# The scores of a chunk in 32 small matrix products of 64 rows by 32 columns instead of 16 of 64 by 64

## The chip, the cores and the metric

The kernel runs on one core of a Trainium2 chip. A core has a matrix engine (TensorE; PE in the profile, with PEld for its weight loads), three engines for element work (VectorE is DVE, ScalarE is ACT, GpSimd is POOL), and DMA queues, here issued by SyncE (SP). Matrix products read both operands from on-chip memory and write to PSUM, which has eight banks. The metric is device microseconds of a whole execution, lower is better; the median of several runs is given.

TensorE's array is 128 rows by 128 columns. A product whose stationary operand is smaller uses a part of it, called a place below: 64 rows by 64 columns makes four places, 64 rows by 32 columns eight. Which place a product takes follows from the partitions of its operands (rows) and of its result (columns). Products in different places can run at the same time. Each 32-bit product is issued as two passes, and each pass is one weight load and one matmul in the profile, so the counts of the profile are twice those of the code.

## The reference, cut to what matters

A decayed scan over 768 positions (4 batches, 8 heads, head size 32, state size 16) is followed by a feed-forward part. What the change touches is the scores `CB`:

```python
log_a = np.log(np.clip(a, 1e-06, 1.0))
for c in range(nc):
    cum = np.cumsum(la, axis=-1)
    L = np.exp(cum[:, :, :, None] - cum[:, :, None, :]) * causal
    CB = np.einsum('bhin,bhjn->bhij', Cc, Bc)
    M = CB * L
    y_intra = np.einsum('bhij,bhjd->bhid', M, xc)
    y_inter = np.einsum('bhin,bhnd->bhid', Cc, state) * decay_to_i[:, :, :, None]
    y[:, :, sl] = y_intra + y_inter
    state = decay_full[:, :, None, None] * state + np.sum(Bx, axis=2)
...
x = y.transpose(0, 2, 1, 3).reshape(B * S, H * D)
a = x @ w1
b = x @ w2
return (a * b @ w3) @ w_out
```

## The kernel before, in words

The scan runs over 16 chunks of 48 positions (`T = 48`). The state's 16 rows and a chunk's 48 positions are put together into blocks of 64 rows, so that one product per head gives the output and the next state at once. A chunk c has these steps on the engines:

- `c.CB`: the scores. 16 products, each with 64 rows (two heads' B with the unit matrix, zero elsewhere) and 64 of the 128 columns of a packed tile `bc`, against 96 columns of C. Row half r goes to PSUM bank `b[r]`; each product fills 64 partitions and 96 columns of it. In the profile: `ps<-bc`, 64*64, 32 matmuls.
- `c.M0`, `c.M1`: VectorE multiplies the two banks by the decays and leaves the result in `r`.
- `c.MX`: the sums, x and decays: 32 products of 64 rows by 32 columns, `r` against `xe`, 64 columns each. In the profile: `ps<-r,xe`, 64*32, 64 matmuls.
- `c.hi`, `c.lo`, `c.T` and `c.Z0` to `c.Z7` take the result out of PSUM: to `xT` for the feed-forward part, and the state's rows into the next chunk's `xe`.

Beside them the feed-forward part runs: `l<slice>.<block>.m` are the products with w1 and w2 (matmuls `ps<-xT,wh` and `ps<-xT,wl` of the whole 128 by 128 array), `v...M` multiplies w3 with w_out (`ps<-fr`), `d....m` are the last products (`ps<-wo,fr`). Products of 512 zeros (`ps<-zero`, the words with a `+`) fill TensorE early on.

The order of all work on every engine is written out by hand in the table `PLAN` (lines 25 to 82): each word is a task, with its engine behind a colon and its PSUM banks behind an @. Every operation is pinned to that order, by helpers on lines 134 to 150, so all matmuls show as L135 in the profile. In that order six `CB` stand right behind an `MX` on TensorE, three right in front of one, three behind another `CB`, and four between other products.

Of the kernel before, what the change touches and what calls it, by code (L numbers as in the profile page):

```python
# [85 lines left out]
def kernel(  # L86
# [17 lines left out]
    P = 128  # L104
# [18 lines left out]
    _, NST, NMAG, _, NOB, NCT, NR, NPK = 28, 4, 5, 11, 2, 2, 2, 3  # L123
# [7 lines left out]
    def sb(shape, dtype, name):  # L131
        return const.tile(shape, dtype, name=name)

    def mm(*args, **kw):
        pin(nc.tensor.matmul(*args, **kw))  # L135

    def load(dst, src, e="D"):
        pin((nc.scalar if e == "S" else nc.sync).dma_start(dst, src))  # L138
# [14 lines left out]
    psum = [PS[:, i] for i in range(8)]  # L153
# [23 lines left out]
    zero = sb([P, 512], BF16, "zero")  # L177
# [33 lines left out]
    tasks = {}  # L211

    def task(name):
        def put(f):
            tasks[name] = f
            return f
        return put
# [49 lines left out]
    def chunk(c):  # L267
# [3 lines left out]
        def step(name):  # L271
            return task(f"c{c}.{name}")
# [17 lines left out]
        if c < DIRECT:  # L290
            if c >= TRI:
                @step("K")
                def _(e, b):
                    q, k = divmod(c, SQ // T)
                    src = cq[q, :, :, :, k * T:(k + 1) * T]
                    load(LD.bitcast(F32)[RJ:, :, N:], src.rearrange("h g t s -> (g t) h s"), e)
                    for h2 in range(2):
                        load(RD.bitcast(F32)[RI + 2 * h2:RI + 2 * h2 + 2], src[h2].rearrange("g t s -> t g s"), e)
# [35 lines left out]
        def half(i):  # L334
            return psum[i][:, :HG * T]
# [14 lines left out]
            step(f"W{hf}")(lambda e, b, hf=hf: bw(hf))  # L350
            step(f"M{hf}")(lambda e, b, hf=hf: weigh(hf))

        @step("CB")
        def _(e, b):
            for r in range(2):
                v["pc", r] = half(b[r]).rearrange("p (g s) -> p g s", s=T)
            for k in range(4):
                for r in range(2):
                    rows = slice(64 * r, 64 * r + 64)
                    for i in range(2):  # L360
                        cols = slice(64 * i, 64 * i + 64)
                        mm(psum[b[r]][cols, 2 * T * k:2 * T * (k + 1)], bq[rows, k, cols], bq[rows, k, P:],
                           start=True, stop=True)


        @step("MX")
        def _(e, b):
            assert b[1] == b[0] + 1
            py = v["py"] = PS[:, b[0]:b[0] + 2].rearrange("p c (j k m) -> p (c j) k m", j=2, k=KT)[:, :, :, :TE]
            for kt in range(KT):  # L370
                for j in range(2):
                    for i in range(2):
                        for q in range(4):
                            n = 2 * (i ^ (q & 1)) + j
                            g = n * HP + 2 * kt + q // 2
                            rows = slice(64 * i, 64 * i + 64)
                            mm(py[32 * q:32 * q + 32, n, kt, :], xe[rows, g], R[rows, g, :], start=True, stop=True)

        if c + 1 < NCH:
            @step("T")  # L380
# [38 lines left out]
    for c in range(NCH):  # L419
        chunk(c)  # L420
# [165 lines left out]
            down(sl, t, vs)  # L586

    for word in PLAN.split():
        name, _, banks = word.partition("@")
        name, _, engine = name.partition(":")  # L590
        b = [int(i) for i in banks.split(",")] if banks else []
        if name[0] == "+":
            for _ in range(int(name[1:])):
                mm(psum[b[0]], zero[:, 0:P], zero, start=True, stop=True)
        else:
            tasks.pop(name)(engine, b)
    assert not tasks, list(tasks)


# [73 lines left out]
```

## Time and profile before

| | us |
|---|---|
| median of 3 runs (lowest to highest) | 276.61 (275.95 to 276.85) |
| the profiled execution's own time | 277.0 |
| its span in the profile | 275.2 |
| TensorE busy with matmuls (3024) | 267.5 (97%) |
| TensorE busy with weight loads (3026) | 236.6 |
| VectorE busy | 171.1 |
| ScalarE busy | 112.6 |
| GpSimd busy | 103.0 |

The 277.0 us of the profiled execution are 1.8 us more than its span, for start and end, and 0.4 us above the median. In rows of the timeline the first number is the start in us from the span's start, the second the time from there to the end of the last instruction of the row, so that the next row may start before it ends; xN is the number of matmuls in it. The granted clock was full (1.0) for the whole span.

### The profile page before, as it was taken

To read this page: it belongs to the slowest core of one execution; us is meant where nothing else is said; L and a number is where in the kernel's file an instruction comes from. 1 tells how busy PE (TensorE), PEld (TensorE's weight loads), DVE (VectorE), ACT (ScalarE), POOL (GpSimd) and SP (SyncE) were. 2 spreads that over 40 slices of the span, in tenths; PEclk is the share of its full clock that TensorE was granted. 3 is DMA by queue.
4 is the path that set the end of the run, shared out by engine and by line. 5 is a ranking of instruction groups with operands and counts; after the bars stand their busy time and mean duration, and the time that the engine had idled before them with its cause. 6 is when DMAs were issued, how large, how long until landed. Compare 5 with 4: busy or idle time off the path is not lost.

```text
span 275.2 us, 7389 instructions
## 1 busy us (share of the span) xinstructions
PE 267.5 (97%) x3024; PEld 236.6 (86%) x3026; DVE 171.1 (62%) x339; ACT 112.6 (41%) x242; POOL 103.0 (37%) x139
## 2 busy tenths in 40 slices
PE   8989999999999998999999999999999999999994
PEld 2459999999788897988988989988898899899994
DVE  4389997898896979988537462184447404441260
ACT  4484687755655442365143142042525212220220
POOL 3232527526445335465426061042416603250100
PEclk9999999999999999999999999999999999999999
DMA  6999979995983872606008100100211001000101
GB/s 193 344 272 318 307 254 319 269 293 161 376 247 111 289 249 79 182 0 183 18 23 243 48 21 0 50 28 0 63 58 39 2 27 52 0 0 23 39 19 40
DMA packets 21755, 36.05 MB, mean 131 GB/s; under 512 B 3672, under 2 KB 13528, under 8 KB 21720
## 3 DMA queue, kind: packets, MB, share of 16 engines
q1 hardware_dynamic: 21720, 35.56, 41.2%
q8 instruction: 24, 0.39, 0.6%
q14 instruction: 11, 0.09, 0.1%
HBM read 32.11 MB, written 3.44 MB: 129 GB/s over the span
## 4 chain that ended last, share of the span: by engine, by line
PE 88%; DMA 5%; DVE 2%; SPq 2%; issue 1%; ACT 0%
PE ps L135 88%; DMA xe<-in_x_dram 3%; SPq L138 2%; DMA st<-in_w3t_dram 1%; DMA st<-in_w_dram 1%; DVE mag L450 1%; DVE st L144 0%; DVE xT L141 0%; ACT xT L147 0%; DVE fr L141 0%; ACT gs L147 0%; DVE ob L147 0%; DVE wh L147 0%; DVE fr L147 0%; DVE gs L141 0%
## 5 line engine op out<-in xcount | busy, mean ns | idle before, releaser
L135 PE MATMUL ps<-xT,wh 128*128 128x512 f32 (+2 forms) x448 | 124.7, 362 | 1.0 <-DVE xT L141 1.0
L135 PEld LDWEIGHTS ps<-xT,wh 128*128 128x128 f32 x448 | 79.8, 188 | 11.5 <-DVE xT L141 1.0
L135 PE MATMUL ps<-xT,wl 128*128 128x512 f32 (+2 forms) x224 | 80.4, 359 | 0.0
L135 PE MATMUL ps<-wo,fr 128*128 128x256 f32 x576 | 69.7, 281 | 0.0
L135 PEld LDWEIGHTS ps<-wo,fr 128*128 128x128 f32 x576 | 68.7, 189 | 0.7
L141 POOL TENSOR_TENSOR fr<-gs,fr 128x512 fp32r<-128x512 f32 (+2 forms) x30 | 38.0, 1283 | 79.0 <-PE ps L135 29.0
L147 ACT COPY gs<-ps 128x512 f32<-128x512 f32 (+2 forms) x56 | 29.4, 524 | 65.1 <-PE ps L135 63.4
L141 DVE TENSOR_TENSOR gs<-gs,ps 128x512 f32<-128x512 f32 (+2 forms) x56 | 33.8, 608 | 33.8 <-PE ps L135 26.2
L135 PEld LDWEIGHTS ps<-xT,wl 128*128 128x128 f32 x224 | 42.2, 188 | 5.2
L147 DVE CAST fr<-gs 128x512 fp32r<-128x512 f32 (+2 forms) x29 | 13.4, 471 | 25.3 <-PE ps L135 24.7
L135 PE MATMUL ps<-fr 128*128 128x256 f32 x192 | 25.5, 286 | 0.8 <-DVE fr L141 0.8
L135 PEld LDWEIGHTS ps<-fr 128*128 128x128 f32 x192 | 24.1, 190 | 1.8 <-DVE fr L141 1.0
L141 POOL TENSOR_TENSOR fr<-mag,fr 128x512 fp32r<-128x512 f32 x11 | 15.9, 1445 | 17.9 <-DVE fr L147 14.8
L147 ACT COPY ob<-ps 128x256 f32<-128x256 f32 x16 | 6.0, 374 | 40.0 <-PE ps L135 34.7
L150 ACT ACTIVATE mag<-st 128x512 f32<-128x512 f32 x28 | 18.6, 674 | 8.2 <-DVE fr L141 5.4
L147 POOL COPY xe<-z 16x128 f32<-16x128 f32 x42 | 13.8, 330 | 20.1 <-DVE z L382 13.9
L141 POOL TENSOR_TENSOR r<-bn,r 128x128 f32<-128x128 f32 x32 | 16.0, 516 | 13.8 <-ACT r L150 8.5
L141 DVE TENSOR_TENSOR fr<-gs,fr 128x512 fp32r<-128x512 f32 (+2 forms) x26 | 19.5, 765 | 1.1 <-ACT fr L147 0.9
L450 DVE SCALAR_TENSOR_TENSOR mag<-mag,st 128x512 uint32<-128x512 uint32 x28 | 19.8, 717 | 0.2
L144 DVE TENSOR_SCALAR st<-st 128x512 uint32<-128x512 uint32 x28 | 14.5, 520 | 6.2 <-DMA st<-in_w_dram 4.1
L147 ACT CAST fr<-gs 128x512 fp32r<-128x512 f32 (+2 forms) x27 | 13.8, 559 | 10.5 <-PE ps L135 8.0
L141 DVE TENSOR_TENSOR r<-ps,r 128x384 f32<-128x384 f32 x32 | 16.6, 551 | 1.6 <-POOL r L141 0.8
(52 smaller groups left out, 209.8 us busy)
## 6 DMA issues: line engine op xcount, KB each, us to landing
st<-in_w3t_dram SPq DMA_DIRECT2D x16, 512.0 KB, 4.9
bc<-in_Ct_dram SPq DMA_DIRECT2D x14, 448.0 KB, 8.5
xe<-in_x_dram SPq DMA_DIRECT2D x16, 256.0 KB, 4.5
st<-in_w_dram SPq DMA_DIRECT2D x16, 256.0 KB, 6.2
ct<-cd SPq DMA_DIRECT2D x16, 192.0 KB, 6.2
out_dram<-ob SPq DMA_DIRECT2D x24, 128.0 KB, 2.1
st<-in_w_out_dram SPq DMA_DIRECT2D x4, 512.0 KB, 6.0
bn<-in_Bn_dram SPq DMA_DIRECT2D x14, 128.0 KB, 4.4
```

Of the source, the lines that this page charges most:

```text
L135: pin(nc.tensor.matmul(*args, **kw))
L138: pin((nc.scalar if e == "S" else nc.sync).dma_start(dst, src))
L141: pin((nc.gpsimd if e == "G" else nc.vector).tensor_tensor(*args))
L144: pin(nc.vector.tensor_scalar(*args))
L147: pin(nc.scalar.copy(*args) if e == "S" else (nc.gpsimd if e == "G" else nc.vector).tensor_copy(*args))
L150: pin(nc.scalar.activation(*args, **kw))
L450: pin(nc.vector.scalar_tensor_tensor(d, m, 3, v["wl"].bitcast(U32), ALU.logical_shift_left, ALU.bitwise_or))
```

## The change

The products of `CB` become twice as many with half as many columns each: four column places `q` of 32 columns take the place of two of 64. The rows, the 96 streamed columns, the banks and the sum of what is written are the same. The functions of `CB` and `MX` become generators (`scores`, `sums`), and the loop over `PLAN` learns to run words that are joined by `&` in turns; the table `PLAN` itself is the same and has no such word, so each generator is run to its end at its old place.

```diff
-                    for i in range(2):
-                        cols = slice(64 * i, 64 * i + 64)
+                    for q in range(4):
+                        cols = slice(32 * q, 32 * q + 32)
                         mm(psum[b[r]][cols, 2 * T * k:2 * T * (k + 1)], bq[rows, k, cols], bq[rows, k, P:],
                            start=True, stop=True)
-
-
-        @step("MX")
-        def _(e, b):
+                yield
+
+        def sums(b):
...
                             mm(py[32 * q:32 * q + 32, n, kt, :], xe[rows, g], R[rows, g, :], start=True, stop=True)
+                    yield
+
+        step("CB")(lambda e, b: scores(b))
+        step("MX")(lambda e, b: sums(b))
...
     for word in PLAN.split():
...
+        turn = []
+        for part in word.split("&"):
...
+            else:
+                turn.append(tasks.pop(name)(engine, b))
+        turn = [g for g in turn if hasattr(g, "__next__")]
+        while turn:
+            turn = [g for g in turn if next(g, g) is not g]
```

No instruction changes its place among the others. On TensorE the first place at which `CB` stands right in front of `MX` (chunk 3's scores in tile `bc_80`, then chunk 2's sums from `r_81` and `xe_74`), in the order of issue, where a row is an instruction as the code gives it, with its result's partitions by columns:

```order
 L135 MATMUL ps<-xT_85,wh 128x384
 L135 MATMUL ps<-xT_84,wl 128x384
-L135 MATMUL ps<-bc_80 64x96 x16
+L135 MATMUL ps<-bc_80 32x96 x32
 L135 MATMUL ps<-r_81,xe_74 32x64 x32
 L135 MATMUL ps<-xT_84,wh 128x384
```

The sixteen products of 64 columns became thirty-two of 32 columns, with the same two neighbours, one of them of the form that they now have.

On TensorE the first place at which two `CB` (chunks 7 and 8) follow each other, behind chunk 6's `MX`:

```order
 L135 MATMUL ps<-rd,ld 128x384 x2
 L135 MATMUL ps<-r_81,xe_74 32x64 x32
-L135 MATMUL ps<-bc_80 64x96 x16
-L135 MATMUL ps<-bc_79 64x96 x16
+L135 MATMUL ps<-bc_80 32x96 x32
+L135 MATMUL ps<-bc_79 32x96 x32
 L135 MATMUL ps<-xT_84,wh 128x512
```

Here three groups of small products follow each other, and now all three have one form.

More of the change, by code (lines that the diff above doesn't have):

```diff
@@ L351, in chunk, with scores @@
             step(f"M{hf}")(lambda e, b, hf=hf: weigh(hf))
-        @step("CB")
-        def _(e, b):
+        def scores(b):
             for r in range(2):
@@ L359, in _ @@
                     rows = slice(64 * r, 64 * r + 64)
-                    for i in range(2):
-                        cols = slice(64 * i, 64 * i + 64)
+                    for q in range(4):
+                        cols = slice(32 * q, 32 * q + 32)
                         mm(psum[b[r]][cols, 2 * T * k:2 * T * (k + 1)], bq[rows, k, cols], bq[rows, k, P:],
                            start=True, stop=True)
-        @step("MX")
-        def _(e, b):
+                yield
+        def sums(b):
             assert b[1] == b[0] + 1
@@ L588 @@
     for word in PLAN.split():
[L589 to L596, printed above, removed]
+        turn = []
+        for part in word.split("&"):
+            name, _, banks = part.partition("@")
+            name, _, engine = name.partition(":")
+            b = [int(i) for i in banks.split(",")] if banks else []
+            if name[0] == "+":
+                for _ in range(int(name[1:])):
+                    mm(psum[b[0]], zero[:, 0:P], zero, start=True, stop=True)
+            else:
[3 more added lines that the diff above has]
+            turn = [g for g in turn if next(g, g) is not g]
     assert not tasks, list(tasks)
```

## The prediction

> **What bounds the kernel now.** I read first the page (busy shares and the chain of waits), then TensorE's timeline around the scores (CB) and the sums (MX), then the timeline inside one MX, and last the places where the chain leaves TensorE.
>
> ```profile
> PE 267.5 (97%) x3024; PEld 236.6 (86%) x3026; DVE 171.1 (62%) x339; ACT 112.6 (41%) x242; POOL 103.0 (37%) x139
> PE 88%; DMA 5%; DVE 2%; SPq 2%; issue 1%; ACT 0%
> ```
>
> TensorE is busy for 97% of the span and carries 88% of the chain that ends last. A CB that gets longer or shorter moves the end by as much, except where the chain is not on TensorE at that time. So I need the length of a CB on TensorE, and the gaps at its two ends. The timeline of TensorE at three of the groups:
>
> ```profile
> 31.50 0.89 PE L135 MATMUL ps<-bc 64*64 64x96 f32 x32
> 32.33 0.86 PE L135 MATMUL ps<-r,xe 64*32 64x64 f32 x64
> 33.11 0.62 PE L135 MATMUL ps<-xT,wh 128*128 128x384 f32 x2
> ...
> 108.11 0.86 PE L135 MATMUL ps<-r,xe 64*32 64x64 f32 x64
> 108.90 0.89 PE L135 MATMUL ps<-bc 64*64 64x96 f32 x32
> 109.72 0.86 PE L135 MATMUL ps<-fr 128*128 128x256 f32 x5
> ...
> 143.81 0.86 PE L135 MATMUL ps<-r,xe 64*32 64x64 f32 x64
> 144.60 1.55 PE L135 MATMUL ps<-bc 64*64 64x96 f32 x64
> 146.08 0.73 PE L135 MATMUL ps<-xT,wh 128*128 128x512 f32 x2
> ```
>
> From start to the next group's start, a CB costs 0.82 us (108.90 to 109.72) and an MX 0.79 (108.11 to 108.90). But two CB together cost 1.48 (144.60 to 146.08), so a CB that follows another of its own form costs only 1.48 - 0.82 = **0.66 us**. Its 32 passes go through four places in 8 turns, so a turn takes 0.66 / 8 = 0.0825 us. The other 0.82 - 0.66 = **0.16 us** are the price of a change of form: TensorE runs empty before products of another form start.
>
> **The change part by part.** First, the streaming. Before, 16 products in 4 places are 4 products for a place, each of two passes; after, 32 products in 8 places are again 4 products for a place, with the same 96 columns to stream. Eight turns of 0.0825 us remain. At the start a weight load of 32 columns in place of 64 is shorter. These rows of the two tiles give the lengths (least, median, most, in ns):
>
> ```profile
> L135 PE MATMUL ps<-r,xe x1024: 212/216/240, 12.4 to 212.2; 64*32 64x64 f32 x171
> L135 PE MATMUL ps<-bc x512: 242/243/294, 9.6 to 199.2; 64*64 64x96 f32 x171
> ```
>
> The longest matmuls are the first ones, which stand waiting for their weights: 24 ns more with 32 columns (240 - 216), 51 ns more with 64 (294 - 243). So the first turn gets 0.027 us shorter; but eight places start one after the other and not four, 0.007 us apart (32 passes in 0.245 us, below), which ends the last turn 4 x 0.007 = 0.028 later. Together nothing.
>
> Second, the supply of instructions, which doubles to 64 passes, 128 instructions with the loads. MX has just that number in just these eight places. TensorE's timeline cut at 32.57, 32.60, 32.74, 32.89 and 32.97 (each row counts the MX matmuls started by then; the first row is the loads by 32.57):
>
> ```profile
> 32.33 0.30 PEld L135 LDWEIGHTS ps<-r,xe 64*32 64x32 f32 x33
> 32.33 0.46 PE L135 MATMUL ps<-r,xe 64*32 64x64 f32 x32
> ...
> 32.33 0.48 PE L135 MATMUL ps<-r,xe 64*32 64x64 f32 x33
> ...
> 32.33 0.64 PE L135 MATMUL ps<-r,xe 64*32 64x64 f32 x40
> ...
> 32.33 0.79 PE L135 MATMUL ps<-r,xe 64*32 64x64 f32 x58
> ...
> 32.33 0.86 PE L135 MATMUL ps<-r,xe 64*32 64x64 f32 x64
> ```
>
> 32 matmuls and their loads, 64 instructions, start in 0.245 us without a pause. The 33rd matmul then comes alone at about 32.59, 0.26 us after the first, and from there they come at (58 - 40) per 0.15 us, 8.3 ns each or 17 ns for a product of two passes. I read this so: no more than 64 instructions are out at a time, and the 65th goes out only when the earliest have ended; the first matmul lasts 0.24 us, and a further 0.02 to 0.03 pass until its successor starts. The Trainium skill, "TensorE: Matmul & The Clock Gate", Engine queue depths, gives TensorE a queue of 64 entries; the trace agrees with its count (33 loads and 32 matmuls by 32.57), and by a queue of 64 a CB before, with its 64 instructions, would never show this pause.
>
> Walked through for the new CB, whose matmul lasts 0.243 us, 0.267 with its first load: the first place is free for its third product at 0.027 + 4 x 0.0825 = 0.357 us after the start, and that product can be out at 0.267 + 0.03 = 0.30, in time. The second place's third product takes the entries behind it, which come free when the first place's second pass ends: start 0.027 + 0.0825 = 0.11, end 0.35, so out at 0.38; its place was free at 0.364, and its load of 0.027 is no longer hidden: it streams from 0.41, 0.045 late. The places behind come free 0.007 apart but get their products 0.017 apart, so the eighth is 0.045 + 6 x 0.010 = **0.11 us** late. In the fourth products nothing more is lost, since a place needs one each 0.165 us and eight are supplied in 8 x 0.017 = 0.134. Bounds: 0, if a turn of 0.0825 covers the pause wholly, and 0.17, MX's own pause (its 64 passes end at 0.64 us; eight turns at the first half's pace, 0.08 + 6 x 0.055 + 8 x 0.007, would end at 0.47). I take 0.11, as the walk gives it.
>
> For the second CB of a pair, which starts with 64 instructions already out: a product holds its four entries for 0.0825 + 0.243 + 0.03 = 0.355 us, and 0.38 with an unhidden load; 16 products out at a time are then 8 per 0.178 to 0.19 us where the places could take 8 per 0.165. Four such rounds lose 0.05 to 0.10; I take 0.07.
>
> Third, the junctions. With one form, MX and CB follow each other as two CB do now, so up to 0.16 us each go; the lower bound is nothing. Six MX stand right before a CB (48.36, 67.80, 108.11, 122.59, 143.81, 197.08) and three CB right before an MX (31.50, 37.85, 56.78). The Trainium skill, "TensorEngine Tiling (Array Packing)", Key Properties, says that changing the tiling mode, not just the tile, drains TensorE; by it 64 by 32 after 64 by 32 has no drain, and the pair at 144.60 agrees. An MX behind a CB loses its 64 prepared instructions: 32 passes at 8.3 ns, 0.27, instead of 0.245, so +0.02 for each of three. Some first products behind a junction wait on several semaphores, for which the program has wait instructions of their own in TensorE's queue (31.50, 56.78, 122.59, and between the two CB at 144.60). They were read far ahead; now there is no lead. Their cost is not in the trace: from 0 to the whole 0.16 of the junction each. I take 0.04 each, near the low end, since a semaphore that is long set should hold little.
>
> Fourth, what of this lies on the chain. The chain in order of time:
>
> ```profile
> 5.51 7.51 DMA xe<-in_x_dram
> 13.04 2.96 DMA st<-in_w_dram
> 16.01 1.83 PE ps L135 x57
> ...
> 65.55 3.89 DMA st<-in_w3t_dram
> 69.45 0.28 ACT xT L147
> 69.76 0.15 DVE xT L141
> ```
>
> Until 16.01 transfers set the time, so the CB of chunks 0 and 1 (9.56, and 14.36 below) are covered. The second is followed by fill that waits 0.33 us for ScalarE. The cover of the first is thinner: MX behind it waits for VectorE, which waits for this CB; without the transfers it would cost its 0.11. Near 68 us the chain is on ScalarE and VectorE:
>
> ```profile
> 14.36 0.89 PE L135 MATMUL ps<-bc 64*64 64x96 f32 x32
> 15.58 1.46 PE L135 MATMUL ps<-zero 128*128 128x512 bf16 x5 [0.33 <-ACT r L150]
> ...
> 67.80 0.86 PE L135 MATMUL ps<-r,xe 64*32 64x64 f32 x64
> 68.59 1.55 PE L135 MATMUL ps<-bc 64*64 64x96 f32 x64
> 70.53 0.69 PE L135 MATMUL ps<-xT,wh 128*128 128x512 f32 x2 [0.38 <-DVE xT L141]
> ```
>
> Both CB at 68.59 lie beside the way from MX over ScalarE and VectorE to 70.53, with 0.38 us to spare; what they lose or gain there counts nothing. There remain 10 CB at 0.11, 2 second CB at 0.07, and 8 junctions:
>
> 10 x 0.11 + 2 x 0.07 + 3 x 0.02 + 4 x 0.04 - 8 x 0.16 = 1.10 + 0.14 + 0.06 + 0.16 - 1.28 = **+0.18 us**.
>
> On the profiled execution's 277.0 that is 277.2; on the median, 0.4 lower, 276.61 + 0.18 = **276.8**. Less than 0.3% (0.83 us) can't be told from no change in this kernel, so the forecast is no change. Nothing moves on other engines. VectorE gets the scores up to 0.11 us later or 0.16 earlier, and the one MX that waited for it is the covered one:
>
> ```profile
> PE ps L135 <- DVE r L141: 0.7, 1, 0.7
> q8 instruction: 24, 0.39, 0.6%
> ```
>
> The second row is the fetching of all 7389 instructions; 1024 more are a seventh of it, 0.1% of the DMA engines' time, which I cost at nothing beside transfers of 41%.
>
> **The rivals.**
>
> *The pause doesn't show, the junctions do (faster).* For it: a place needs a product only each 0.165 us, and the supply gives eight in 0.134. Against it: the pause in MX is there although the pace behind it would do. Time: 276.61 - 1.28 = 275.3. Chance 0.17.
>
> *The junctions stay (slower).* If TensorE runs empty for another reason than the form (another number of columns, other banks, the wait instructions), each of the 8 junctions keeps its 0.16, and the supply's loss stands alone: 1.10 + 0.14 = 1.24, 277.9. For it: the only pair without a gap in the trace is CB behind CB, alike in everything; and the two large forms 128 by 128 follow each other without a gap whatever their columns, which is against it. It decides (more than 0.83 us) once a junction gives less than about 0.08. Chance 0.15.
>
> *The eight places don't work side by side with 96 columns.* Then the passes stream one half after the other, 0.66 us more for each of 12 CB, 276.61 + 7.9 = 284.5. Against it stand MX's 32 matmuls of over 0.2 us each within 0.245. Chance 0.02.
>
> One page speaks for a loss still larger: the Trainium skill, "TensorE: Matmul & The Clock Gate", under "Wait — 56ns, not 53.3ns?", says that starts are never closer than about 25 ns however few the columns; by it 64 passes would take 1.6 us and the change would cost 12 x 0.78 = 9 us. The trace contradicts it: the 64 of MX take 0.79. I give it no chance of its own.
>
> **How the numbers follow.** No change 0.66, faster 0.17, slower 0.15 + 0.02 = 0.17. The forecast's own range is 275.8 to 277.4, that is within 0.3% of before. The range of 8 in 10 reaches to both larger rivals, whose outer halves are left out: 275.2 to 278.0.
>
> **What would show it right or wrong.** In the changed profile: MX to CB groups (108.11 to 109.72, now 1.61 us) should take about 1.61 - 0.16 + 0.11 = 1.56, and CB to MX (31.50 to 33.11) the same or a little more; a CB between other forms (21.79, 93.38) about 0.93 instead of 0.82, with 32 of its 64 matmuls started without a pause and the 34th late; the group at 143.81 (2.27 us now) within 0.1 of that. Groups of 1.45 and a CB of 0.82 speak for the first rival, groups of 1.7 for the second. A CB of 1.4 us or more, or a change on another engine, would make the prediction wrong altogether.

## The result: slower by 1.1%

| | before | changed |
|---|---|---|
| median (lowest to highest), us | 276.73 (275.95 to 276.92), 4 runs | 279.85 (278.49 to 280.51), 4 runs |
| the profiled execution, us | 277.0 | 278.49 |
| its span, us | 275.2 | 276.7 |

The ratio is 1.0112, 95% interval 1.0085 to 1.0139. The forecast of no change, 276.8 us, was wrong, and the time lies above the range's end of 278.0. The changed kernel also scatters more: 2.0 us between its runs, 1.0 before. Ratios, here and below, leave out runs more than 1.5% above the fastest of their kernel, so they can be smaller than the quotient of the medians.

From the page of the changed kernel, its busy line, its chain and the DMA queue that brings the instructions:

```profile
PE 267.8 (97%) x3536; PEld 237.6 (86%) x3538; DVE 171.8 (62%) x339; ACT 112.8 (41%) x242; POOL 102.3 (37%) x139
PE 85%; DMA 6%; DVE 3%; issue 2%; SPq 1%; ACT 1%; DVEq 0%; ACTq 0%
q8 instruction: 28, 0.46, 0.7%
```

TensorE's busy time is up by 0.3 us only, although it has 512 more matmuls. What grew is "issue", the time in which an engine waited for nothing that the profile shows: from 1% of the chain to 2%. The view of TensorE's waits (us in total, times, longest), and all rows of its timeline after 10 us that stand behind such a wait:

```profile
PE ps L135 <- issue: 2.4, 3, 1.5
...
15.49 1.04 PE L135 MATMUL ps<-zero 128*128 128x512 bf16 x4 [0.61 <-issue]
69.30 1.11 PE L135 MATMUL ps<-bc 64*32 64x96 f32 x67 [0.33 <-issue]
200.52 0.40 PE L135 MATMUL ps<-bc 64*32 64x96 f32 x15 [1.48 <-issue]
```

Before, the list of TensorE's waits had no row for issue. Now TensorE stands still three times, and all three waits are on the chain that ended last. The first is among the fill products, the other two are inside pairs of scores: in the last pair, 113 of the 128 matmuls run, then nothing starts, then the other 15 follow with no semaphore between them. (The bracket counts from the end of the matmul before; from start to start the gaps are 0.98, 0.57 and 1.72 us.)

Most else went as the sum had it. TensorE's timeline of the changed kernel at a lone CB, at the group of 108 us, and at the pairs of 144 and 197 us:

```profile
21.29 0.99 PE L135 MATMUL ps<-bc 64*32 64x96 f32 x64
22.21 0.63 PE L135 MATMUL ps<-xT,wh 128*128 128x384 f32 x2
...
107.85 0.80 PE L135 MATMUL ps<-r,xe 64*32 64x64 f32 x60
108.43 0.27 PE L135 MATMUL ps<-bc 64*32 64x96 f32 x1
...
109.40 0.52 PE L135 MATMUL ps<-fr 128*128 128x256 f32 x2
...
143.48 0.80 PE L135 MATMUL ps<-r,xe 64*32 64x64 f32 x60
...
145.82 0.50 PE L135 MATMUL ps<-xT,wh 128*128 128x512 f32 x1
...
196.82 0.80 PE L135 MATMUL ps<-r,xe 64*32 64x64 f32 x60
197.40 0.26 PE L135 MATMUL ps<-bc 64*32 64x96 f32 x1
...
200.85 0.62 PE L135 MATMUL ps<-wo,fr 128*128 128x256 f32 x3
```

The lone CB takes 0.92 us (0.82 before; 0.93 was written). The group of 108 us takes 1.55 (1.61 before; 1.56 was written), and the scores now start among the last sums: the junction is gone. The pair of 144 us takes 2.34 (2.27 before). The pair of 197 us has the same instructions as that of 144 and takes 4.03 (2.26 before): 1.77 us lost in one place. All that stands between 16.5 us and this pair loses 0.25 together: the changed kernel is 0.51 us ahead at 16.46 and 0.26 ahead at 196.82.

### The profile page after: what moved, and what is told of

Read it like the earlier page. It is cut to its first block, busy times and chain, and to the rows that moved or that the text cites. A ratio compares the mean times of both kernels' runs of the same rounds, so it can differ in the third digit from the quotient of the medians.

```text
span 276.7 us, 8413 instructions
## 1 busy us (share of the span) xinstructions
PE 267.8 (97%) x3536; PEld 237.6 (86%) x3538; DVE 171.8 (62%) x339; ACT 112.8 (41%) x242; POOL 102.3 (37%) x139
## 4 chain that ended last, share of the span: by engine, by line
PE 85%; DMA 6%; DVE 3%; issue 2%; SPq 1%; ACT 1%; DVEq 0%; ACTq 0%
PE ps L135 85%; DMA st<-in_w3t_dram 2%; DMA st<-in_w_dram 2%; DMA st<-in_w_out_dram 1%; DVE mag L454 1%; SPq L138 1%; DVE st L144 1%; ACT xT L147 1%; ACT xe L147 0%; DVE gs L141 0%; DVE fr L141 0%; DVE r L141 0%; DVE z L386 0%; DVE fr L147 0%; DVE xT L141 0%
## 5 line engine op out<-in xcount | busy, mean ns | idle before, releaser
L147 DVE CAST fr<-gs 128x512 fp32r<-128x512 f32 (+2 forms) x29 | 14.2, 497 | 25.3 <-PE ps L135 24.7
L141 POOL TENSOR_TENSOR r<-bn,r 128x128 f32<-128x128 f32 x32 | 15.0, 481 | 12.8 <-ACT r L150 9.3
L135 PE MATMUL ps<-bc 64*32 64x96 f32 x1024 | 16.0, 248 | 1.8 <-issue 1.8
```

Source lines behind the costliest of these rows:

```text
L141: pin((nc.gpsimd if e == "G" else nc.vector).tensor_tensor(*args))
L147: pin(nc.scalar.copy(*args) if e == "S" else (nc.gpsimd if e == "G" else nc.vector).tensor_copy(*args))
```

## The theory after the result

Theory A: TensorE runs out of instructions. The page has 24 packets of instructions before and 28 now, for 1024 instructions more: 256 to a packet. They fit TensorE's own instructions, of which the traces have 6100 and 7124 (24 x 256 = 6144, 28 x 256 = 7168). I numbered TensorE's instructions (matmuls, weight loads, waits) by their start in the trace; the first one behind each of the three gaps has the number 448, 2495 and 5823, which is 192, 191 and 191 beyond a multiple of 256. So each gap stands at the end of a block of 256, and what is missing is the next block. A group of sums and two scores had 256 instructions in 2.27 us, and now has 384 in 2.4 us if nothing stops it: more than a whole block, with no slow matmul in it, so that a block can be asked for and used up within one group. Whether that happens depends on where in the group the block ends, hence one pair stalls and its twin at 144 us does not.

The Trainium skill, "Runtime: NRT & Kernel Launch", Instruction fetch mechanics, says that instructions come in blocks of 16 KiB, 256 of them, the next one fetched while the current one runs, and that the cost of the boundary is mostly hidden. The traces agree on the 256 (254 to a packet, from 6100 in 24 and 7124 in 28), and show that here the cost is not hidden (0.52 to 3.75 us at a gap).

Theory B, the rival: the loss is in the eight places themselves (the queue in front of TensorE, PSUM, the work of the pair), and stays with them wherever a block ends.

## The experiments

Ratios are against the kernel before, run on the same chip in the same batch (276.3 to 276.6 us).

### Eight places only in chunks 14 and 15, and the same shifted by 112 instructions

```diff
 (both, in the changed kernel)
-                    for q in range(4):
-                        cols = slice(32 * q, 32 * q + 32)
+                    w = 32 if c in (14, 15) else 64
+                    for q in range(P // w):
+                        cols = slice(w * q, w * q + w)
 (the second one also)
-                for _ in range(int(name[1:])):
-                    mm(psum[b[0]], zero[:, 0:P], zero, start=True, stop=True)
+                n = 8 if word == "+8@5" else 1
+                for _ in range(n * int(name[1:])):
+                    mm(psum[b[0]][:, :512 // n], zero[:, 0:P], zero[:, :512 // n], start=True, stop=True)
```

All chunks but these two go back to four places, as before. The second cuts the first 8 fill products, far ahead of all chunks, into 64 with an eighth of the columns.

> The kernel before with the eight places in chunks 14 and 15 alone, the pair near 198 us. Theory A: here a block ends 29 instructions ahead of the group and the next one 227 behind its start, so that the block in between is asked for well ahead; no stall over 0.3 us, 276.3 to 277.0 us. Theory B: that pair is as in the changed kernel, so 1.7 us of stall stand in it, 278 to 278.7 us.

> The eight places in chunks 14 and 15 alone, and the first 8 fill products cut into 64, 112 instructions more ahead of the chunks. Theory A: now a block is asked for right where the group begins and is used up within it: a stall of 1 to 2 us inside the group near 198 us, 277.7 to 279 us, 1 to 2 us above the same kernel without the cut. Theory B: the same time as without the cut.

Without the shift: 276.71 us, ratio 1.0018 (0.9995 to 1.0041). With it: 279.5 us, ratio 1.011 (1.0073 to 1.0147). The last pair in the timeline of the first, then of the second:

```profile
197.24 0.80 PE L135 MATMUL ps<-r,xe 64*32 64x64 f32 x60
...
197.90 1.72 PE L135 MATMUL ps<-bc 64*32 64x96 f32 x126
199.55 2.21 PE L135 MATMUL ps<-wo,fr 128*128 128x256 f32 x17
```

```profile
197.33 0.80 PE L135 MATMUL ps<-r,xe 64*32 64x64 f32 x60
...
197.99 1.64 PE L135 MATMUL ps<-bc 64*32 64x96 f32 x119
201.15 0.37 PE L135 MATMUL ps<-bc 64*32 64x96 f32 x7 [1.52 <-issue]
201.45 0.39 PE L135 MATMUL ps<-wo,fr 128*128 128x256 f32 x1
```

The same products take 2.31 us in the first and 4.12 in the second, and ahead of them only the cut of the fill products differs, which moves the place of a block's end. The stall is at number 5057, 193 beyond a multiple of 256. Theory B falls for this pair. The medians are 2.8 us apart, more than the 1 to 2 that theory A had expected, and the second is above its 279; the two profiled executions are 2.2 us apart, of which the stall explains 1.8.

### The kernel before, shifted

Only the cut of the fill products, nothing else.

> The kernel before, with only its first 8 fill products cut into 64 (112 instructions more ahead of the chunks, no product of the chunks changed). Theory A: groups of sums and two scores in four places are 256 instructions, and the slow matmuls behind them give the next block time wherever its end falls; no wait of TensorE on issue of over 0.3 us after 20 us, 276.2 to 277.2 us. Theory B (the cut itself costs the 3 us seen with chunks 14 and 15): 279 us or more.

276.72 us, ratio 1.0012 (0.9996 to 1.0027). One wait on issue of 0.2 us is left in its view of waits. So the cut costs nothing by itself, and in the kernel with four places the ends of blocks do not hurt where the cut puts them either.

### The changed kernel again

No edit.

> The changed kernel once more, for a second profile of an execution. Theory A: waits on issue at the same places of the program (within the pair near 69 us and within the pair near 199 us), at the same number of instructions, but of other lengths, since it is a transfer that is late; 278.5 to 281 us.

280.21 us (279.34 to 282.61), ratio 1.0153 (1.0114 to 1.0193). In the profiled execution, of 279.97 us, the gap in the last pair is at number 5825 as before (193 beyond a multiple of 256), and 2.19 us long from start to start instead of 1.72. The pair near 69 us did not stall at all this time, where the first profile had 0.57; that part of the expectation missed. The places at which a stall can stand are fixed by the program; whether it comes, and how long it is, varies from one execution to the next, as it can with a transfer. That is one reason why the executions scatter.

### The changed kernel, shifted

The cut of the fill products in the changed kernel, run twice under two names.

> The changed kernel with its first 8 fill products of 512 columns cut into 64 of 64 columns: the same streaming, 112 instructions more ahead of all chunks, so the ends of the blocks of 256 fall 112 instructions earlier in the program. Theory A: the stall between the two scores near 199 us goes (under 0.3 us), one of 1 to 2 us comes in the pair near 145 us, and the pair near 69 us keeps a stall of 0.3 us or more; 277.5 to 280.5 us in all. Theory B: the waits stay where they are, near 69 and 199 us, with the same 0.6 and 1.7 us.

> The changed kernel with its first 8 fill products cut, once more, since the profile of the first look shows an execution of 1460 us whose every matmul is some six times as long. Theory A: stalls of over 0.3 us in the pairs near 69 and 145 us and none near 199 us; 284 to 292 us, as the other executions before had.

The first time: 284.89 to 291.87 us in five executions (ratio 1.0354, from 1.0305 to 1.0404), far above the 277.5 to 280.5 that theory A had expected; the profiled sixth took 1460 us with matmuls some three to four times as long (1510 ns in place of 367 for `ps<-xT,wh`), and nothing is read from it. The second time: 287.63 us (two executions), ratio 1.0408 (1.0373 to 1.0442). Its waits, the rows behind the longest of them up to 80 us, and the one in the pair that stands near 145 us in the changed kernel:

```profile
PE ps L135 <- issue: 6.9, 6, 2.4
...
34.31 0.30 PE L135 MATMUL ps<-r,xe 64*32 64x64 f32 x2 [1.77 <-issue]
63.30 0.76 PE L135 MATMUL ps<-fr 128*128 128x256 f32 x5 [0.52 <-issue]
78.00 0.50 PE L135 MATMUL ps<-xT,wh 128*128 128x512 f32 x1 [2.37 <-issue]
...
154.37 0.39 PE L135 MATMUL ps<-bc 64*32 64x96 f32 x13 [1.78 <-issue]
```

As expected the pair near 199 us is free of it and the pair near 145 us (now at 150) has a gap, of 2.02 us from start to start. Against the expectation the pair near 69 us has none; the products right behind it stall (78.00), and two places that I had not foreseen: sums behind a single CB (34.31), and matmuls of `fr` behind such a group (63.30). The loss is larger than the waits: see the clock, below.

### The pairs in four places, and the same shifted

```diff
-                    for q in range(4):
-                        cols = slice(32 * q, 32 * q + 32)
+                    w = 32 if c not in (7, 8, 12, 13, 14, 15) else 64
+                    for q in range(P // w):
+                        cols = slice(w * q, w * q + w)
```

> The change in 10 of the 16 chunks; the six scores that stand in pairs (chunks 7, 8, 12, 13, 14, 15) keep four places. Theory A (TensorE runs out of instructions: they are fetched in blocks of 256, and sums and two scores of 64 passes each use a block up before the next is there): no wait of TensorE on issue of over 0.3 us after 20 us, lone scores still 0.93, and 276.4 to 277.3 us, no change against before. Theory B (the loss is in the eight places themselves, wherever they stand): 10 of 16 chunks changed, so some 60% of the loss stays, 278 to 279 us.

> Eight places in the 10 chunks whose scores stand alone or beside sums only, the three pairs in four places, with the first 8 fill products cut. The same products as in the run without the cut, which stood still for 3.5 us behind the sums near 69 us, where a block ends 7 instructions ahead of the group. Theory A: with the cut that end lies 119 instructions ahead of the group, the block is asked for in time, and the stall goes: 276.3 to 277.5 us and no wait on issue over 0.5 us after 20 us. Theory B (the eight places of the other chunks cost): 278 to 279 us as without the cut.

279.24 us (276.89 to 282.99), ratio 1.006 (1.0033 to 1.0088); shifted 281.94 us, ratio 1.0188 (1.0156 to 1.0219). Both expectations of theory A were too low, and the waits that they excluded are there: I had held a stall possible in the pairs only. The timeline of the first one's profiled execution, of 283 us, and then that of the shifted kernel near 32 us:

```profile
68.85 0.86 PE L135 MATMUL ps<-r,xe 64*32 64x64 f32 x64
69.64 1.54 PE L135 MATMUL ps<-bc 64*64 64x96 f32 x60
74.68 0.58 PE L135 MATMUL ps<-bc 64*64 64x96 f32 x4 [3.51 <-issue]
```

```profile
31.40 0.98 PE L135 MATMUL ps<-bc 64*32 64x96 f32 x63
...
32.20 0.89 PE L135 MATMUL ps<-r,xe 64*32 64x64 f32 x61
34.71 0.30 PE L135 MATMUL ps<-r,xe 64*32 64x64 f32 x2 [1.62 <-issue]
```

The longest stall of all stands in a pair that was left in four places, with the very instructions that it has before. What the change did to it is only the numbering: 448 instructions more stand ahead of it, and now a block ends 7 instructions before the group and the next one at its end. In the shifted kernel that pair is free, and a single CB of eight places with the sums behind it, 256 instructions in 1.55 us, is caught instead. Neither theory B (a loss where the eight places are) nor my narrow form of A holds; the wide form does: any stretch that uses up a block faster than the next one comes can stall, and every instruction added moves all later ends of blocks.

### Eight places in chunks 9 to 14 only

The same edit with `9 <= c < 15`.

> The kernel before with the eight places in chunks 9 to 14 alone: one alone, two right behind sums, a whole pair, and the first of the last pair. By the count of instructions no block of 256 is asked for and used up within one group here. Theory A (only the late blocks cost; the form itself is neutral): no wait of TensorE on issue over 0.3 us after 20 us, chunk 9's scores 0.93 instead of 0.82, sums and scores near 108 us 1.55 instead of 1.61, and 276.3 to 277.0 us, no difference to before. Theory B (each changed chunk costs its share of the 3 us): 6 of 16 chunks, 277.5 to 278.2 us.

276.83 us (275.82 to 279.94), ratio 1.0026 (1.0001 to 1.0052): at most 0.5% more, with six of sixteen chunks changed, within theory A's range and below theory B's 277.5. Its lone CB and its group near 108 us in the timeline:

```profile
93.54 1.00 PE L135 MATMUL ps<-bc 64*32 64x96 f32 x64
94.47 0.74 PE L135 MATMUL ps<-fr 128*128 128x256 f32 x4
...
107.90 0.80 PE L135 MATMUL ps<-r,xe 64*32 64x64 f32 x60
...
109.45 0.74 PE L135 MATMUL ps<-fr 128*128 128x256 f32 x4
```

0.93 and 1.55 us, as written. One wait on issue of 0.4 us stands after 20 us, against the expectation; it is in front of chunk 5's sums, at 57.76 us, which are not changed there, on an instruction that waits on a semaphore, and not at a block's end. What released it stays open; gaps of 0.3 to 0.5 us at the same sums appear in three other profiles.

### All gaps together

Every gap of 0.5 us or more, from start to start, after 12 us and ahead of an instruction that waits on no semaphore, in all profiles but the one of 1460 us:

| kernel | number of the first instruction behind the gap, its remainder by 256, gap in us |
|---|---|
| before; before shifted; chunks 9 to 14 | none |
| changed | 448: 192, 0.98; 2495: 191, 0.57; 5823: 191, 1.72 |
| changed again | 449: 193, 1.30; 5825: 193, 2.19 |
| changed, shifted | 1217: 193, 1.99; 2241: 193, 0.80; 2753: 193, 2.77; 3777: 193, 0.52; 4801: 193, 2.02 |
| pairs in four | 449: 193, 1.69; 2497: 193, 3.75 |
| pairs in four, shifted | 1217: 193, 1.84; 2241: 193, 1.84 |
| chunks 14 and 15 | 449: 193, 0.78 |
| chunks 14 and 15, shifted | 5057: 193, 1.77 |

Sixteen gaps, in seven executions of six different kernels, at one remainder (the count can be off by a record or two that a trace lacks). A seventeenth, of 0.67 us at number 1985 (193) of the pairs in four, shifted, is left out of the table because its instruction also waits on a semaphore.

The traces also record when each packet of instructions was moved. Before the end of each of the sixteen gaps, and of the seventeenth, stands one such packet: it begins 2.3 to 2.9 us and has ended 1.2 to 1.4 us before TensorE starts again, whether the gap is 0.52 us long or 3.75. At the wait of 57.76 us, which is not at a block's end, the last packet had ended 6.6 us earlier. That the gaps are the fetch of instructions in blocks of 256 is shown by the remainder, by the packets and by the shifts.

How fast a block is used up decides whether it can stall. The ten profiles have 249 ends of blocks that can be timed. Of the 23 blocks whose instructions all started within 3.5 us, 15 had such a gap behind them; of the 16 between 3.5 and 5 us, 1; of the 210 slower ones, none.

## Why the prediction was wrong, step by step

**The step that failed** is the last sentence of the change's part: "1024 more are a seventh of it, 0.1% of the DMA engines' time, which I cost at nothing". The share of the queue is small (0.6% became 0.7%), but it is not throughput that counts. A block must come before the one in hand is used up, and I never set the time of a block against the time in which TensorE goes through 256 instructions. In the changed kernel's last pair the packet of the next block was moved from 198.17 to 199.12 us, and its first instruction ran at 200.52, 2.35 us after the transfer had begun. Without a stall the group goes through its 384 instructions at 6.3 ns each (the 2.4 us above), 256 in 1.6 us. The price is 1.77 us in this one pair, and 2.23 by the second profile. The prediction took the row for the fetching of all 7389 instructions; its 24 packets fit TensorE's own 6100 alone, 254 to a packet, and one such packet was never set against a group of sums and two scores, which had 256 instructions in 2.27 us.

**The pause of the supply within a CB** was right: 0.92 us for the 0.93 written. In the trace of that CB the first 32 passes start at full pace and the later ones behind it, as in MX. A lone CB loses 0.10 us (0.11 written).

**The junctions** were right: -0.16 each, with 1.55 us in place of 1.61 for groups of MX and CB, 1.56 written. This also settles the second rival: TensorE ran empty because of the form.

**The wait instructions at junctions** were mis-sized at one place of four. Where two of them stand between a CB and an MX, the group became longer:

```profile
31.13 1.00 PE L135 MATMUL ps<-bc 64*32 64x96 f32 x64
31.99 0.96 PE L135 MATMUL ps<-r,xe 64*32 64x64 f32 x64
32.87 0.62 PE L135 MATMUL ps<-xT,wh 128*128 128x384 f32 x2
```

1.74 us (1.61 before; the like groups without them 1.55), so 0.19, slightly more than the upper bound of 0.16 and far more than the 0.04 taken. At the other three the trace shows 0.00 to 0.03. In the second profile of the same kernel the first of these groups takes 1.62 us (at 32.47), and the one before the `fr` products 2.00 (at 57.67), with a wait of 0.22 on issue in front of its sums, 4.5 us after the last packet of instructions had ended. So the size of this term varies between executions, and what sets it stays open.

**The sum without the stalls.** The groups on the chain give 2 x 0.10 (lone), +0.13 (31.13), -0.06 x 4 (the CB to MX at 38 and 57 us, the MX to CB at 48 and 108), -0.03 (123 us) and +0.07 (the pair of 144 us): +0.13, where +0.16 had been written for the same groups (the +0.18 less 0.02 for the last pair). So the terms that were sized give the right sum, in part by luck: the group at 31.13 lost 0.12 more than written and most others 0.01 to 0.07 less. The stall of 1.77 in one pair is ten times that sum. The pair near 69 us did not stay beside the way: the time from its start to the matmul behind it went from 2.73 to 2.95 us, 0.22 lost through the stall of 0.57.

**From the profiled +1.5 us to the +3.1 us of the medians.** The first profile is of the shortest of the four executions. The second one, of 279.97 us, is near the medians (279.85 and 280.21), 3.0 us above the profiled execution before. The sums of chunk 1 before, then its scores and sums in the first profile of the changed kernel, and in the second profile the same with the fill between, and the last pair:

```profile
16.97 0.86 PE L135 MATMUL ps<-r,xe 64*32 64x64 f32 x64
```

```profile
13.29 1.00 PE L135 MATMUL ps<-bc 64*32 64x96 f32 x64
...
16.46 0.86 PE L135 MATMUL ps<-r,xe 64*32 64x64 f32 x64
```

```profile
14.10 1.00 PE L135 MATMUL ps<-bc 64*32 64x96 f32 x64
...
16.84 1.04 PE L135 MATMUL ps<-zero 128*128 128x512 bf16 x4 [0.93 <-issue]
17.81 0.86 PE L135 MATMUL ps<-r,xe 64*32 64x64 f32 x64
...
197.84 0.80 PE L135 MATMUL ps<-r,xe 64*32 64x64 f32 x60
...
202.00 0.40 PE L135 MATMUL ps<-bc 64*32 64x96 f32 x15 [1.95 <-issue]
202.33 0.84 PE L135 MATMUL ps<-wo,fr 128*128 128x256 f32 x5
```

Before, the scores of chunk 1 start at 14.36. In the first profile they happen to start 1.07 us earlier, and the stall among the fill behind them takes 0.56 back; with 0.2 in the pair near 69 us and 1.77 in the last pair that is the +1.5, and all else cancels. In the second profile they start only 0.26 earlier, the stall among the fill costs 1.10, and the last pair takes 4.49 us in place of 2.26, so 2.23: together the +3.0. So the stalls at the ends of blocks account for the profiled executions, one of them near the median; no longer execution of this kernel has a profile, and that those scatter by the same gaps is only argued.

**The rivals.** None of them named the fetch. Of the chance of 0.17 for slower, 0.15 was put on junctions that would stay, and these went, and 0.02 on places that do not work side by side, and they do.

## What to carry to other kernels

Small products in more places double the instructions, and TensorE's instructions come in blocks of 256: count how long it takes through any 256 of them in a row, and where that is under some 3.5 us, as in the 23 blocks above, expect a stall that comes and goes with the place at which a block ends. An edit that adds or takes instructions moves every later end, so a group can stall that was never touched; compare such edits at several offsets. Groups of one array form next to each other save 0.16 us at each junction, which is real and far less than one late block (0.5 to 3.75 us here).

## What the runs showed of the hardware that was not expected

**The granted clock halves behind some of the stalls.** In the shifted changed kernel, the row of the granted clock over 40 slices of 7.1 us, then windows behind three of its stalls (start and end, length, TensorE busy, its clock, DMA share, GB/s):

```profile
PEclk9999979999999999999998899999999999999999
...
35.70:39.11 3.41, 3.41 (x12) 0.50 0.87 284
39.11:43.00 3.89, 3.89 (x142) 1.00 0.21 46
155.16:158.58 3.42, 3.42 (x10) 0.50 0.75 209
...
78.00:90.00 12.00, 12.00 (x118) 1.00 0.67 186
```

The clock is at half for one stretch of 3.41 us, which begins 1.4 us behind the stall that ends at 34.31 and 0.8 us behind the one that ends at 154.37, both 2.0 us long. Half of 2 x 3.41 us, 3.4 us, are lost to it beside the 6.9 us of waits (an estimate): 276.3 + 6.9 + 3.4 = 286.6, and the execution took 287.2. Behind the longest stall of the same execution, the 2.77 us that end at 78.00, the clock stays full, and so it does behind the 2.19 us of the changed kernel's second profile. In the pairs in four, such a stretch begins at 74.45 us, at the end of the 3.75 us. So the length of a stall alone does not decide it, and what does stays open.

**Why the first third of the kernel is hit hardest** stays open. DMA engines were 86% busy from 15.5 to 69.25 us and 36% from 69.3 to 199 in the changed kernel, and in the first stretch even 256 instructions in 1.55 us next to slow matmuls stalled. The packets show where the time goes: once a packet has begun, TensorE starts again 2.3 to 2.9 us later, early and late in the kernel, but ahead of the gaps before 80 us it began up to 4.1 us behind the first instruction of the block in hand, and ahead of the later gaps at most 1.2 us behind it. That a busy DMA delays the block fits this, but no run changed the traffic alone.
